# Two sums of output weights and all stores of plain gating weights placed in tile zero; GpSimd's sums cut into pieces of 256 columns and placed earlier

## The chip, the cores and the metric

The kernel runs on one core of a Trainium2 chip. The metric is the device time of one execution in microseconds; the time of a kernel is the median of its timed runs. One further execution of the kernel was taken by the hardware profiler, and all views of a profile below are of that one execution.

## What is computed

Attention inside chunks of 64 tokens (8 batches, 8 heads, 576 tokens of 64), then RMS norm and a SwiGLU layer over the 4608 tokens of 512 numbers:

```python
scores = scale * np.matmul(q_c, k_c.transpose(0, 1, 2, 4, 3))      # within a chunk
attn = softmax(scores);  out = np.matmul(attn, v_c)                # x: 4608 x 512
xn = x / rms * rms_g
g = xn @ w_gate                                                    # 512 x 1536
silu = g * (1.0 / (1.0 + np.exp(-g)))
val = xn @ w_val
return (silu * val @ w_out).astype(np.float32)                     # 1536 x 512
```

The weights arrive as 64-bit words and are made into float32 on the chip. Every matrix product is done in two-part numbers: each operand is split into a high and a low part, and three products of parts (high by high, high by low, low by high) are summed.

## The kernel before

**Tiles.** The 4608 tokens are nine tiles of 512. Tiles 0, 1 and 2 are computed plainly: for each of the 12 blocks `f` of 128 hidden units, 12 matmuls make the gate, 12 the value, SiLU and a product follow, and later the down product. Tiles 3 to 8 are taken in pairs by a seven-product scheme (`P1` to `P7`), which needs sums and differences of weight blocks; these are made once, stored in DRAM, and loaded again by each pair. Tile 0 keeps the names `acc`, `ps_g`, `ps_v` of its own; tiles 1 and 2 are one loop whose down products also use the seven-product scheme (`down_pair` with `b` = -1).

**What has to be prepared for the pairs.** There are six weight groups `i` (`NPR` = 6), each with three preparations:

- `save_up(i)` (L678) stores three plain weight blocks of the up side as they are: three DMAs of 512 KB from `parts` to the DRAM tensor `wsd`, all on SyncE's queue.
- `sides(i)` makes the four sums of the up side in a tile `ab`. It returns six functions, called at the half-steps `SIDE_AT[i] + SIDE_STEPS`: `whole` and `sums` on GpSimd (both through `total`, L693), then twice a `split` (two casts on ScalarE, `side`, L716, and two differences on VectorE, L717) and a `save` (four DMAs of 256 KB).
- `out_sides(i, home)` makes the sums of the output weights in a tile `w` and writes them back into `out_parts[i]`: `sums` (L657 and four L665, VectorE), `parts` (cast on ScalarE, L669; difference on VectorE, L670) and `store` (two DMAs of 512 KB to `wol`). They are called at `SUM_AT[i] + SUM_STEPS`.

**Attention ahead.** While tiles 1 and 2 are multiplied, the attention of units 4 to 9 (256 tokens each) is done in steps placed by `UNIT_AT`: load of queries and keys (`qk`, one buffer), scores on TensorE (L269), softmax (L341, L342, L348, L353 to L362), a trip of the exponentials through DRAM (`away_e`, then `eT`, one buffer), values on TensorE (L394), norm (`xu`, L408; the square on ScalarE, L464, which writes into `eT`; `ms` and `ri_t` on GpSimd, L466 and L467; L419) and a trip of the result through DRAM (`away_x`, back into `x`). At the turn from tile 1 to tile 2, L521 (ScalarE) and L522 (VectorE) split `x` into `xh` and `xl`.

**What sets the order.** Tile 0 is put in order by a scheduler with priorities. From tile 1 on the engines execute in the order in which the code is written: in tiles 1 and 2 there are 48 half-steps (two for each `f`), and a table gives the half-step at which a function is called. Every engine, and SyncE's queue of DMAs, takes its instructions strictly in turn. SyncE has eight semaphores for DMAs in turn, so each DMA also waits until the one issued eight before it has landed.

**Buffers.** The weight tiles, `ab` and the big `g` tiles share a pool of 18 buffers (`wts`), all of which the converted weights fill at the end of tile 0. The first buffer that comes free is that of `out_parts[0]`, when its `wol` store has landed; the first `ab` tile goes there.

Of the kernel before, what the change touches and what calls it, by code (L numbers as in the profile page):

```python
# [8 lines left out]
F32 = mybir.dt.float32  # L9
# [5 lines left out]
ALU = mybir.AluOpType  # L15
AX = mybir.AxisListType

P = 128
# [10 lines left out]
DM = 512  # L29
NDT = DM // P  # L30
DFF = 1536
NF = DFF // P
# [15 lines left out]
)  # L48
SIDE_AT = 6, 11, 15, 25, 29, 33
SIDE_STEPS = 0, 2, 4, 5, 6, 7  # L50
SUM_AT = 0, 3, 6, 11, 26, 32
SUM_STEPS = 0, 1, 3
SAVE_AT = 19, 22, 27, 31
LAST_HOME = 42
WO_AT = 36, 42
SPLIT_AT = 41, 45
# [13 lines left out]
KH = DM // 2  # L70
# [20 lines left out]
for p in DOWN:  # L91
    todo = [(p, i) for i in range(NPR)]
# [9 lines left out]
def tile_chunk_attn_swiglu(  # L102
# [40 lines left out]
    wp = last.open("wp", 3)  # L143
# [99 lines left out]
    def load_values(u):  # L243
        vt = io.tile([P, NPAIR, UT // CH, D], F32, tag="io", name="vt")
        nc.sync.dma_start(vt, v[u])
        for s in range(2):
            state[2 * u + s]["v"] = vt
# [280 lines left out]
    def behind(ins):  # L528

        info = mybir.DependencyInfo(mybir.DependencyClass.Sync, mybir.DependencyReason.DATA)  # L530
        tc.add_manual_dep(ins.ins, split_last[0].ins.name, info, reason="tokens are split first")
        return ins
# [114 lines left out]
    def out_sides(i, home):  # L647

        hi, lo = (out_parts[i][:, n].rearrange("p f (h c) -> p (f h) c", c=KH) for n in range(2))
        slots = wol_.rearrange("p (k i) (a c) -> p i a k c", i=NPR, a=2)[:, i]  # L650
        hi32, lo32 = hi.bitcast(F32), lo.bitcast(F32)
        ws = []

        def sums():
            w = home().tile([P, 4, KH], F32, tag="ab", bufs=1, name="w")
            ws.append(w)
            nc.vector.tensor_tensor(w, hi32, lo32, op=ALU.add)  # L657
            a11, a21, a12, a22 = (w[:, n] for n in range(4))
            for o, one, two, op in (
                (a22, a21, a22, ALU.add),  # L660
                (a21, a11, a21, ALU.subtract),
                (a11, a22, a11, ALU.subtract),
                (a12, a12, a11, ALU.subtract),
            ):
                nc.vector.tensor_tensor(o, one, two, op=op)  # L665

        def parts():
            w = ws[0]
            nc.scalar.copy(hi, w)  # L669
            nc.vector.tensor_tensor(lo, w, hi32, op=ALU.subtract)  # L670

        def store():
            for a, part in enumerate((hi32, lo32)):
                nc.sync.dma_start(slots[:, a], part)

        return [sums, parts, store]

    def save_up(i):  # L678

        for f, ps in enumerate(((P1, P2), (P4,))):  # L680
            part = conv_parts[2 * i + f].bitcast(F32).rearrange("p a m (h c) -> p h (a m) c", h=2)
            for h, p in zip((0, 1) if f == 0 else (1,), ps):
                nc.sync.dma_start(wsd[:, 7 * i + p].rearrange("p (n c) -> p n c", c=KH), part[:, h])
# [4 lines left out]
    def sides(i, st):  # L688

        at, ws = {}, []  # L690

        def total(out, one, two, op):
            return nc.gpsimd.tensor_tensor(out, one, two, op=op)  # L693

        def whole():
            ws = big([P, 2, 2, DM], F32, "ab")
            for f in range(2):
                hi, lo = (conv_parts[2 * i + f][:, n].bitcast(F32) for n in range(2))
                behind(total(ws[:, f], hi, lo, ALU.add))
                for half in range(2):  # L700
                    at[f + 1, half + 1] = ws[:, f, :, half * KH : (half + 1) * KH]

        def sums():
            total(at[2, 2], at[2, 1], at[2, 2], ALU.add)
            total(at[2, 1], at[1, 1], at[2, 1], ALU.subtract)
            total(at[1, 1], at[2, 2], at[1, 1], ALU.subtract)
            total(at[1, 2], at[1, 2], at[1, 1], ALU.subtract)

        forms = ((P7, (2, 1)), (P5, (2, 2))), ((P6, (1, 1)), (P3, (1, 2)))
        parts = {}  # L710

        def split(k):
            for p, n in forms[k]:
                w = at[n]
                part = parts[p] = st().tile([P, 2, KH], F32R, tag="side", bufs=4, name="side")
                nc.scalar.copy(part, w)  # L716
                nc.vector.tensor_tensor(w.bitcast(F32R), w, part.bitcast(F32), op=ALU.subtract)  # L717

        def save(k):
            for p, n in forms[k]:  # L720
                dst = wsd[:, 7 * i + p].rearrange("p (a m c) -> p a m c", a=2, m=2)
                nc.sync.dma_start(dst[:, 0], parts[p].bitcast(F32))
                nc.sync.dma_start(dst[:, 1], at[n])

        return [whole, sums, lambda: split(0), lambda: save(0), lambda: split(1), lambda: save(1)]

    def big(shape, dtype, name):
        return wts.tile(shape, dtype, tag="wts", name=name)
# [389 lines left out]
    for f in range(NF):  # L1118
        g = gated(f, CONVS[f % 2], conv_step)
        if f in (0, 5):  # L1120
            u = 2 + (f == 5)
            load_unit(u)
            load_values(u)
            sc = two_banks(ps_a, "ps_s")
            for i in (2 * u, 2 * u + 1):
                scores(i, sc)
            softmax_rows(u, sc)
        elif f in (2, 7):
            for i in (2 * u, 2 * u + 1):
                att_transpose(i)  # L1130
        elif f in (3, 8):
            o = two_banks(ps_a, "ps_o")
            for i in (2 * u, 2 * u + 1):
                att_values(i, o)
            norm_unit(u, o)
        if f % 2:
            save_out(f // 2)
        if f >= 10:
            save_up(f - 10)
        if f == NF - 1:  # L1140
            load_unit(4)
            x_transpose((0, 1))
        if prev is not None:
            down(acc, f - 1, *prev)
        prev = g
# [11 lines left out]
    st = [last.open("st", 1)]  # L1157
    xx = [x, None]
    at, down_at, wos, gs = {}, {}, {}, []
# [3 lines left out]
    def do(k, f):  # L1163
        if k >= 4 * NF:
            down_at.setdefault(2 * (k - 4 * NF), []).append(f)
        else:
            at.setdefault(max(k, 0), []).append(f)
# [12 lines left out]
    for n, u in enumerate(range(4, 10)):  # L1180
        todo = unit_steps(u, lambda n=n: xx[n >= 4])
# [3 lines left out]
    for i in range(NPR):  # L1185
        for k, f in zip(SIDE_STEPS, sides(i, lambda: st[0])):
            do(SIDE_AT[i] + k, f)
        for k, f in zip(SUM_STEPS, out_sides(i, lambda: st[0])):
            do(SUM_AT[i] + k, f)
        do(P5_AT[i], lambda i=i: less_first(i))  # L1190
        if i > 1:
            do(SAVE_AT[i - 2], lambda i=i: save_up(i))
    do(LAST_HOME, last_home)
    for n, k in enumerate(WO_AT):
        do(k, lambda n=n: wo_first(n))
# [3 lines left out]
    half = Steps(at)  # L1199
    room = []  # L1200
    for t in range(1, PLAIN):
        for f in range(NF):
            n = (t - 1) * NF + f
            if n < 4:
                tag = "gh" if n < 2 else "gl"
# [16 lines left out]
    for b in range(-1, NB):  # L1222
        t = PLAIN + 2 * b
        last_pair = b == NB - 1
        if b >= 0:
            at, down_at, wos, gs = {}, {}, {}, []
# [102 lines left out]
```

## Time and profile before

| | us |
|---|---|
| three timed runs | 921.89, 922.05, 923.31 (median 922.05) |
| the profiled execution | 919.45 |
| its span in the profile | 917.6 |
| TensorE busy in the span | 879.9 |
| VectorE / ScalarE / GpSimd busy | 688.9 / 436.7 / 162.5 |

Tile 0 runs to about 145 us, tiles 1 and 2 multiply their up side from there to 316 us, and their down products follow; the three pairs end the span. In a row of the timeline, the columns are the start, the duration of all the instructions in the row, the engine, the line, the operation with output and inputs, the count, and in brackets how long the engine stood idle before the row and what it waited for. In a row of the windows, each engine's busy time stands with its instruction count in brackets, then the clock granted to TensorE (1.00 is full speed), the mean busy share of the DMA engines, and GB/s.

### The profile page before, as it was taken

The page shows a single profiled execution, that of the slowest core. Times are in us where ns is not written, and L with a number is a line of the kernel's source. Part 1 is how long each engine was busy: PE and PEld are TensorE (multiplying, and loading weights), DVE is VectorE, ACT ScalarE, POOL GpSimd, SP SyncE. Part 2 cuts the span into 40 slices and gives each one's busy share as a digit, 9 for nine tenths or more (in the row PEclk, how much of TensorE's full clock was granted, in tenths as well). Part 3 has the DMA queues.
Part 4 walks back from the last instruction along what each step waited for, and adds up shares of the span by engine and source line. Part 5 has one row for each costly group of instructions (what it writes and reads, how often), then busy time and mean ns, then how long its engine had stood idle before and what let it go on. Part 6 is the DMA issues. An engine that isn't in the chain of part 4 may idle for free.

```text
span 917.6 us, 17117 instructions
## 1 busy us (share of the span) xinstructions
PE 879.9 (96%) x6792; PEld 719.4 (78%) x6792; DVE 688.9 (75%) x1083; ACT 436.7 (48%) x733; POOL 162.5 (18%) x153
## 2 busy tenths in 40 slices
PE   5799999979999999999999999999999999999998
PEld 4588878757777788888888788888878888888886
DVE  6999966878799597776666997776669874344885
ACT  5997944244444564333444654344446532212452
POOL 0100000276485100022221000221220002211000
PEclk9999999989999999999999999999999999999999
DMA  9698423759998997578888885688798867445623
GB/s 362 265 375 321 146 92 115 227 199 324 343 370 272 314 335 278 185 263 269 312 259 276 288 304 211 244 283 314 244 294 265 308 250 300 142 150 193 226 66 119
DMA packets 96513, 231.82 MB, mean 253 GB/s; under 512 B 7344, under 2 KB 63664, under 8 KB 81072
## 3 DMA queue, kind: packets, MB, share of 16 engines
q1 hardware_dynamic: 95376, 230.19, 72.1%
q8 instruction: 54, 0.88, 0.4%
q10 hardware_dynamic: 1056, 0.52, 0.2%
q14 instruction: 27, 0.22, 0.1%
HBM read 171.97 MB, written 58.72 MB: 251 GB/s over the span
## 4 chain that ended last, share of the span: by engine, by line
PE 71%; DVE 14%; ACT 7%; DMA 4%; issue 2%; POOL 1%; SPq 0%; ACTq 0%; DVEq 0%; POOLq 0%
PE ps_c L788 11%; PE ps_b L788 11%; PE ps_a L788 11%; PE ps_a L969 7%; PE ps_b L969 7%; PE ps_c L969 6%; PE ps_d L788 5%; PE ps_d L969 4%; PE ps_v L604 2%; DVE ab L717 2%; PE ps_g L604 2%; PE ps_s L269 1%; PE ps_o L394 1%; ACT e L309 1%; ACT parts L214 1%
## 5 line engine op out<-in xcount | busy, mean ns | idle before, releaser
L888 ACT CAST gh<-g 128x512 fp32r<-128x512 f32 x140 | 81.5, 619 | 75.5 <-PE ps_b L969 21.3
L889 DVE TENSOR_TENSOR gl<-g,gh 128x512 fp32r<-128x512 f32 x140 | 95.0, 686 | 29.7 <-ACT gh L888 28.7
L788 PE MATMUL ps_c<-xp,wr 128*128 128x512 f32 x432 | 104.6, 391 | 0.0
L788 PE MATMUL ps_b<-xp,wr 128*128 128x512 f32 x432 | 104.4, 391 | 0.0
L788 PE MATMUL ps_a<-xp,wr 128*128 128x512 f32 x432 | 103.6, 390 | 0.0
L788 PEld LDWEIGHTS ps_a<-xp,wr 128*128 128x128 f32 x432 | 80.9, 188 | 17.1 <-issue 0.3
L788 PEld LDWEIGHTS ps_c<-xp,wr 128*128 128x128 f32 x432 | 80.6, 188 | 17.1
L788 PEld LDWEIGHTS ps_b<-xp,wr 128*128 128x128 f32 x432 | 80.6, 188 | 16.9
L853 POOL TENSOR_TENSOR g<-c,c 128x512 f32<-128x512 f32 x18 | 23.3, 1294 | 358.3 <-DVE c L849 268.2
L604 PE MATMUL ps_v<-xh,parts 128*128 128x512 f32 x192 | 69.4, 416 | 0.0
L604 PE MATMUL ps_g<-xh,parts 128*128 128x512 f32 x192 | 65.0, 392 | 2.2 <-ACT sg L617 2.2
L969 PE MATMUL ps_a<-gh,wo 128*128 128x512 f32 x176 | 55.8, 389 | 0.0
L969 PE MATMUL ps_c<-gh,wo 128*128 128x512 f32 x160 | 51.1, 391 | 1.4 <-DVE gl L889 1.1
L788 PE MATMUL ps_d<-xp,wr 128*128 128x512 f32 x216 | 51.9, 389 | 0.0
L969 PE MATMUL ps_b<-gh,wo 128*128 128x512 f32 x160 | 50.5, 389 | 0.0
L788 PEld LDWEIGHTS ps_d<-xp,wr 128*128 128x128 f32 x216 | 40.5, 188 | 8.4
L931 DVE TENSOR_TENSOR g<-g 128x512 f32<-128x512 f32 x68 | 46.4, 682 | 0.0
L604 PEld LDWEIGHTS ps_v<-xh,parts 128*128 128x128 f32 x192 | 38.6, 201 | 9.1 <-issue 0.2
L604 PEld LDWEIGHTS ps_g<-xh,parts 128*128 128x128 f32 x192 | 36.0, 188 | 10.4 <-ACT sg L617 2.8
L829 ACT ACTIVATE c<-c 128x512 f32<-128x512 f32 x18 | 11.4, 633 | 67.7 <-DVE c L849 67.6
L838 DVE TENSOR_TENSOR u<-ps_b,p 128x512 f32<-128x512 f32 x36 | 24.0, 684 | 25.2 <-PE ps_b L788 24.0
L348 ACT ACTIVATE e<-e 128x512 f32<-128x512 f32 x28 | 17.5, 631 | 50.0 <-DVE e L342 50.0
(176 smaller groups left out, 1903.3 us busy)
## 6 DMA issues: line engine op xcount, KB each, us to landing
wr<-wsd SPq DMA_DIRECT2D x63, 1024.0 KB, 8.6
qk<-qk_dram SPq DMA_DIRECT2D x17, 1024.0 KB, 6.9
wo<-wol SPq DMA_DIRECT2D x16, 1024.0 KB, 8.4
raw<-w_up_dram SPq DMA_DIRECT2D x12, 1024.0 KB, 13.0
wo<-wod SPq DMA_DIRECT2D x12, 1024.0 KB, 9.8
vt<-v_dram SPq DMA_DIRECT2D x18, 512.0 KB, 6.1
wsd<-parts SPq DMA_DIRECT2D x18, 512.0 KB, 7.9
wo<-wol SPq DMA_DIRECT2D x16, 512.0 KB, 8.2
```

The lines of the kernel that those rows point to most:

```text
L214: nc.scalar.copy(parts[:, 0].rearrange("p i c -> p (i c)"), w)
L348: nc.scalar.activation(e, e, AF.Exp, scale=SCALE)
L604: nc.tensor.matmul(ps[k], a, b[dt], start=(dt == 0 and i == 0), stop=(dt == NDT - 1 and i == 2), skip_group_check=True,)
L717: nc.vector.tensor_tensor(w.bitcast(F32R), w, part.bitcast(F32), op=ALU.subtract)
L788: nc.tensor.matmul(ps, w[:, a, m, cols], xp[:, b, kt], start=start and kt == 0 and i == 0, stop=stop and kt == 1 and i == 2, skip_group_ch ...
L829: nc.scalar.activation(t, t if src is None else src, AF.Silu)
L838: nc.vector.tensor_tensor(kp["u2"], b["b"], kp["p1"], op=add)
L853: nc.gpsimd.tensor_tensor(g[1][1], kp["c22"], kept[0]["c22"], op=mult)
L888: nc.scalar.copy(gh, src)
L889: nc.vector.tensor_tensor(gl, src, gh.bitcast(F32), op=ALU.subtract)
L931: nc.vector.tensor_tensor(out, one, two, op=ALU.subtract)
L969: nc.tensor.matmul(ps[m][INTO[p]], w[:, m, a], parts[c], start=p in FROM and i == 0 and j == 0, stop=p in LAST and i == NPR - 1 and j == 2 ...
```

## The change

Four edits. `EARLY_SUMS` = 2: the whole of `out_sides(0)` and `out_sides(1)` is called in tile 0, at `f` = 9 and 10, with `w` in the pool of the weight conversion. All six `save_up` calls are made in tile 0, at `f` = 6 to 11; before, two were there and four at half-steps 19, 22, 27 and 31. GpSimd's `whole` and `sums` are cut into 256 columns: eight instructions where two of 1024 columns were, and eight where four of 2 x 256 were. `SIDE_AT` moves the six `sides` 5, 5, 4, 10, 4 and 3 half-steps forward, and two of the remaining `out_sides` 3 half-steps.

```diff
-SIDE_AT = 6, 11, 15, 25, 29, 33
+SIDE_AT = 1, 6, 11, 15, 25, 30
 SIDE_STEPS = 0, 2, 4, 5, 6, 7
-SUM_AT = 0, 3, 6, 11, 26, 32
+SUM_AT = 0, 0, 3, 8, 26, 32
 SUM_STEPS = 0, 1, 3
-SAVE_AT = 19, 22, 27, 31
+EARLY_SUMS = 2
...
         def sums():
-            w = home().tile([P, 4, KH], F32, tag="ab", bufs=1, name="w")
+            w = home().rearrange("p (n c) -> p n c", c=KH)
...
-                behind(total(ws[:, f], hi, lo, ALU.add))
                 for half in range(2):
-                    at[f + 1, half + 1] = ws[:, f, :, half * KH : (half + 1) * KH]
+                    cols = slice(half * KH, (half + 1) * KH)
+                    for m in range(2):
+                        behind(total(ws[:, f, m, cols], hi[:, m, cols], lo[:, m, cols], ALU.add))
+                    at[f + 1, half + 1] = ws[:, f, :, cols]
 
         def sums():
-            total(at[2, 2], at[2, 1], at[2, 2], ALU.add)
-            total(at[2, 1], at[1, 1], at[2, 1], ALU.subtract)
-            total(at[1, 1], at[2, 2], at[1, 1], ALU.subtract)
-            total(at[1, 2], at[1, 2], at[1, 1], ALU.subtract)
+            for m in range(2):
+                a = {n: w[:, m] for n, w in at.items()}
+                total(a[2, 2], a[2, 1], a[2, 2], ALU.add)
+                total(a[2, 1], a[1, 1], a[2, 1], ALU.subtract)
+                total(a[1, 1], a[2, 2], a[1, 1], ALU.subtract)
+                total(a[1, 2], a[1, 2], a[1, 1], ALU.subtract)
...
-        if f >= 10:
-            save_up(f - 10)
+        if f >= 6:
+            save_up(f - 6)
+        if f >= NF - 1 - EARLY_SUMS and f < NF - 1:
+            for todo in out_sides(f - NF + 1 + EARLY_SUMS, lambda: wp.tile([P, 2 * DM], F32, name="w")):
+                todo()
...
-        for k, f in zip(SUM_STEPS, out_sides(i, lambda: st[0])):
+        for k, f in () if i < EARLY_SUMS else zip(SUM_STEPS, out_sides(i, lambda: st[0].tile([P, 2 * DM], F32, tag="ab", bufs=1, name="w"))):
             do(SUM_AT[i] + k, f)
         do(P5_AT[i], lambda i=i: less_first(i))
-        if i > 1:
-            do(SAVE_AT[i - 2], lambda i=i: save_up(i))
```

Lines after the first edits are numbered four higher in the changed kernel (L716, L717 become L720, L721). TensorE's order is the same in both.

GpSimd, from the end of tile 0 into tile 1, as a difference of the two orders. `L693` is `total`; `ab<-parts` is `whole`, `ab<-ab` is `sums`; `ms` and `ri_t` belong to the norm of unit 4.

```order
 L512 TENSOR_TENSOR ri_u<-ss_u,mhalf 128x2 x2
-L693 TENSOR_TENSOR ab<-parts 128x1024 x2
+L693 TENSOR_TENSOR ab<-parts 128x256 x8
+L693 TENSOR_TENSOR ab<-ab 128x256 x8
+L693 TENSOR_TENSOR ab<-parts 128x256 x8
 L466 TENSOR_SCALAR ms<-ms 128x1
 L467 TENSOR_TENSOR ri_t<-ms,mhalf 128x1
```

All of side 0 and the first half of side 1 now stand ahead of the norm of unit 4; before, only the first half of side 0 did.

VectorE in tile 1, from the end of the softmax of unit 5 (`L362`) to the norm of unit 4 (`L408`) and on, before:

```order
L362 STREAM_TRANSPOSE e<-e 128x512
L657 TENSOR_TENSOR w<-parts 128x1024
L665 TENSOR_TENSOR w<-w 128x256 x4
L619 TENSOR_TENSOR gl<-ps_v,sg 128x512
L670 TENSOR_TENSOR parts<-w,parts 128x1024
L408 TENSOR_TENSOR xu<-ps_o,rs 128x16x32 x2
L619 TENSOR_TENSOR g<-ps_v,sg 128x512
L425 STREAM_TRANSPOSE xu<-xu 128x1024
```

The same place after:

```order
L362 STREAM_TRANSPOSE e<-e 128x512
L619 TENSOR_TENSOR gl<-ps_v,sg 128x512
L721 TENSOR_TENSOR ab<-ab,side 128x2x256 x2
L408 TENSOR_TENSOR xu<-ps_o,rs 128x16x32 x2
L657 TENSOR_TENSOR w<-parts 128x1024
L665 TENSOR_TENSOR w<-w 128x256 x4
L619 TENSOR_TENSOR g<-ps_v,sg 128x512
L670 TENSOR_TENSOR parts<-w,parts 128x1024
```

The third output sum (`L657`, `L665`, `L670`) no longer stands between the softmax of unit 5 and the norm of unit 4; it is earlier by one place of its kind, since the first two are in tile 0, and the next one stands behind the norm. Two pairs of differences of side 0 (`L721`) have come in ahead of the norm, one of them shown.

VectorE at the end of tile 0, before. `L200`, `L203` and `L220` convert the last weights; `L585` and `L590` are the gate's product and its low part for `f` = 9, 10 and 11.

```order
L200 SCALAR_TENSOR_TENSOR w<-raw,w 128x1024
L585 TENSOR_TENSOR sg<-ps_v,sg 128x512
L203 ISA w<-raw,w 128x2048
L590 TENSOR_TENSOR gl<-sg,gh 128x512
L220 TENSOR_TENSOR parts<-w,parts 128x1024 x2
L585 TENSOR_TENSOR sg<-ps_v,sg 128x512
```

After, from the second of the two `L220`:

```order
L220 TENSOR_TENSOR parts<-w,parts 128x1024
L665 TENSOR_TENSOR w<-w 128x256
L657 TENSOR_TENSOR w<-parts 128x1024
L585 TENSOR_TENSOR sg<-ps_v,sg 128x512
L665 TENSOR_TENSOR w<-w 128x256 x3
L590 TENSOR_TENSOR gl<-sg,gh 128x512
L665 TENSOR_TENSOR w<-w 128x256 x2
L670 TENSOR_TENSOR parts<-w,parts 128x1024
L665 TENSOR_TENSOR w<-w 128x256
L670 TENSOR_TENSOR parts<-w,parts 128x1024
L585 TENSOR_TENSOR sg<-ps_v,sg 128x512
```

Most of the two output sums (an `L657` and an `L665` stand further up) is done around the gate products of `f` = 10 and ahead of that of `f` = 11. On SyncE's queue, the twelve moved `save_up` DMAs stand between the stores of tile 0, the first two ahead of the load of the last raw weights; the four `wol` stores stand ahead of the stores of tile 0's output; and the load of unit 4's queries and keys stands behind nine of the twelve.

## The prediction

> **What bounds the kernel now.** I read the page's head first:
>
> ```profile
> span 917.6 us, 17117 instructions
> PE 879.9 (96%) x6792; PEld 719.4 (78%) x6792; DVE 688.9 (75%) x1083; ACT 436.7 (48%) x733; POOL 162.5 (18%) x153
> ```
>
> TensorE is busy 879.9 of 917.6 us, and the change gives it the same matmuls in the same order. So the time can move only by what TensorE waits, or by matmuls that run slowly. I went through TensorE's timeline for its waits; in the brackets stand the wait ahead of the row and what ended it. Between 145 and 316 us, the up side of tiles 1 and 2, where nearly all of the change lies, these are all of them:
>
> ```profile
> 182.71 0.50 PE L604 MATMUL ps_g<-xh,parts 128*128 128x512 f32 x1 [1.08 <-ACT sg L617]
> 188.59 0.27 PE L394 MATMUL ps_o<-vt,eT 64*32 64x64 f32 x2 [2.88 <-DMA eT<-away_e]
> 189.76 1.58 PE L394 MATMUL ps_o<-vt,eT 64*32 64x64 f32 x126 [0.89 <-DMA eT<-away_e]
> 200.76 0.33 PE L269 MATMUL ps_s<-qk 64*64 64x64 f32 x4 [2.31 <-DVE xu L408]
> 201.45 1.97 PE L269 MATMUL ps_s<-qk 64*64 64x64 f32 x60 [0.36 <-DVE xu L408]
> 217.18 1.35 PE L269 MATMUL ps_s<-qk 64*64 64x64 f32 x64 [2.08 <-DMA qk<-qk_dram]
> 234.32 0.50 PE L604 MATMUL ps_g<-xl,parts 128*128 128x512 f32 x1 [0.26 <-DVE xl L522]
> 270.75 0.33 PE L269 MATMUL ps_s<-qk 64*64 64x64 f32 x4 [1.85 <-DVE xu L408]
> 271.44 1.15 PE L269 MATMUL ps_s<-qk 64*64 64x64 f32 x60 [0.36 <-DVE xu L408]
> 290.58 0.50 PE L604 MATMUL ps_g<-xh,parts 128*128 128x512 f32 x1 [1.15 <-ACT sg L617]
> 307.64 0.27 PE L394 MATMUL ps_o<-vt,eT 64*32 64x64 f32 x2 [0.43 <-DMA eT<-away_e]
> 308.63 1.46 PE L394 MATMUL ps_o<-vt,eT 64*32 64x64 f32 x126 [0.72 <-DMA eT<-away_e]
> ```
>
> They add up to 14.37 us. I name them by place: B at 182.71 (1.08), C at 188.59 (2.88 + 0.89), A at 200.76 (2.31 + 0.36), D at 217.18 (2.08), E at 234.32 (0.26), F at 270.75 (1.85 + 0.36), G at 290.58 (1.15), H at 307.64 (0.43 + 0.72).
>
> Next come the windows behind these waits. After start:end and its length stand the busy times (and counts) of PE, PEld, DVE, ACT and POOL, then the granted clock, the DMA share and GB/s:
>
> ```profile
> 100.00:120.00 20.00, 20.00 (x152) 16.51 (x151) 19.08 (x28) 16.93 (x28) 0.02 (x1) 1.00 0.31 123
> 120.00:140.00 20.00, 18.46 (x85) 15.04 (x85) 12.60 (x16) 7.93 (x12) 1.67 (x1) 1.00 0.13 53
> 189.00:200.00 11.00, 8.70 (x150) 6.85 (x150) 9.90 (x8) 1.64 (x3) 8.95 (x5) 0.84 0.81 277
> 200.00:207.00 7.00, 5.88 (x77) 5.01 (x78) 5.47 (x8) 6.24 (x11) 5.12 (x6) 0.76 0.41 141
> 215.00:223.00 8.00, 5.92 (x78) 4.82 (x78) 7.49 (x13) 1.28 (x3) 5.72 (x5) 0.79 0.91 309
> 270.00:274.00 4.00, 2.89 (x68) 2.48 (x69) 3.86 (x8) 2.41 (x6) 2.21 (x4) 0.86 1.06 372
> 274.00:284.00 10.00, 10.00 (x40) 8.07 (x40) 10.00 (x7) 4.05 (x5) 9.77 (x6) 0.89 0.95 273
> 290.00:296.00 6.00, 5.42 (x24) 4.49 (x25) 5.86 (x14) 2.36 (x5) 0.00 (x0) 1.00 0.87 283
> ```
>
> Behind C, A, D and F, the four waits of 1.85 us or more, the clock was 0.84, 0.76, 0.79 and 0.86 to 0.89; behind G (1.15) it was 1.00. So a longer wait costs a second time. I price it as (1 − clock) × length: C 0.16 × 11 = 1.76, A 0.24 × 7 = 1.68, D 0.21 × 8 = 1.68, F 0.14 × 4 + 0.11 × 10 = 1.66; 6.78 in all. The stretch loses 14.37 + 6.78 = **21.15 us**. No more than that is to be had here.
>
> The Trainium skill (TensorE: Matmul & The Clock Gate, "What's actually happening") has the clock halved only after an idle window of about 3.4 us. By it none of these waits would slow a matmul, and the sum below would be smaller by its clock terms (1.76, 1.68 and two thirds of 1.66), about 4.5 us. The rows above disagree, with 0.76 behind a wait of 2.31 us, and I go by them.
>
> **The change, part by part.** *Two output sums leave tile 1.* VectorE, in tile 1, and what TensorE and SyncE did at that time:
>
> ```profile
> 153.76 1.22 DVE L657 TENSOR_TENSOR w<-parts 128x1024 f32<-128x1024 f32 x1
> 155.00 1.80 DVE L665 TENSOR_TENSOR w<-w 128x256 f32<-128x256 f32 x4
> 157.93 1.23 DVE L670 TENSOR_TENSOR parts<-w,parts 128x1024 fp32r<-128x1024 f32 x1 [0.52 <-ACT parts L669]
> 170.97 2.48 DVE L670 TENSOR_TENSOR parts<-w,parts 128x1024 fp32r<-128x1024 f32 x1 [1.91 <-ACT parts L669]
> 171.75 1.48 PE L394 MATMUL ps_o<-vt,eT 64*32 64x64 f32 x128
> 183.33 1.28 DVE L408 TENSOR_TENSOR xu<-ps_o,rs 128x512 f32<-128x512 f32 x2
> 185.46 1.74 SPq L377 DMA_DIRECT2D eT<-away_e  x4
> 200.02 1.28 DVE L408 TENSOR_TENSOR xu<-ps_o,rs 128x512 f32<-128x512 f32 x2
> ```
>
> Unit 4's attention matmuls end at 173.23, but its norm L408 starts at 183.33, because VectorE, strictly in turn, comes to it only then. One sum costs 1.22 + 1.80 + 1.23 = 4.25 us alone; the second one's L670 took 2.48, and it costs some 5.5. The third moves up into their place, so two of three are gone ahead of the norm: 9.7 us less. In come two pairs of differences, 4 × 0.64 = 2.6. Not all of the rest reaches the norm, since VectorE also waits for the softmax; I take 5 us sooner, 178 (5 to 7). C's load (185.46) follows that norm through ScalarE, so it lands near 183.5 instead of 188.5. Without B's wait TensorE wants it at 184.6: **C goes, and so does B**, whose SiLU waits in the same run of work. That is 1.08 + 3.77 + 1.76 = 6.61.
>
> A waits for the norm of unit 5 (200.02). Ahead of it stood the third sum's L657 and L665, 2.80 and 3.88 us in place of 1.22 and 1.80, beside GpSimd. The norm comes to 190 to 193; TensorE, without C, wants it at about 191.7. I leave half a us of A: 2.67 + 1.68 − 0.5 = 3.85 gone (bounds 0 and 4.35).
>
> *GpSimd's sums in pieces.* The pair of differences L717 beside GpSimd and alone, and GpSimd's groups (count, then busy us and mean ns):
>
> ```profile
> 251.13 2.31 DVE L670 TENSOR_TENSOR parts<-w,parts 128x1024 fp32r<-128x1024 f32 x1
> 257.81 5.25 DVE L717 TENSOR_TENSOR ab<-ab,side 128x512 fp32r<-128x512 f32 x2 [0.61 <-ACT side L716]
> 293.19 1.27 DVE L717 TENSOR_TENSOR ab<-ab,side 128x512 fp32r<-128x512 f32 x2
> ```
>
> ```profile
> 169.96 5.74 POOL L693 TENSOR_TENSOR ab<-parts 128x1024 f32<-128x1024 f32 x2 [48.29 <-DMA wol<-parts]
> 257.31 5.20 POOL L693 TENSOR_TENSOR ab<-parts 128x1024 f32<-128x1024 f32 x2
> L693 POOL TENSOR_TENSOR ab<-ab 128x512 f32<-128x512 f32 x24 | 35.2, 1466 | 1.7
> L693 POOL TENSOR_TENSOR ab<-parts 128x1024 f32<-128x1024 f32 x12 | 31.9, 2677 | 48.6 <-DMA wol<-parts 48.6
> L466 POOL TENSOR_SCALAR ms<-ms 128x1 f32<-128x1 f32 x28 | 8.9, 318 | 88.4 <-ACT eT L464 86.9
> ```
>
> Two differences take 1.27 us alone and 5.25 beside a pair of GpSimd sums of 5.20: VectorE is held until GpSimd's instruction is over. A side now costs GpSimd 2 × 2.68 + 4 × 1.47 = 11.2 us. After, it is 16 pieces: 0.67 each (2677 / 4) if nothing is paid per instruction, 0.91 if the 0.32 of a one-column instruction is paid each time; 10.7 to 14.6 a side. I take 0.73 (1466 / 2), 11.7. So GpSimd's own work grows by 0.5 us a side; it is idle 48 us ahead of its first sum, and that sum, waiting for the `wol` store, is able to start near 145 instead of 169.96, since those stores move into tile 0.
>
> The Trainium skill (SBUF — State Buffer, "Who interferes with whom") says that the ports which these two share are locked for a whole instruction and the second to come waits it out. The trace agrees (5.25 beside 5.20). By that rule a piece caps VectorE's wait at about 0.7 us.
>
> In tile 2 F hangs on a chain on VectorE from 247 to the norm at 270.02, with 5.25 for 1.27 and 2.31 for 1.23 in it: up to 5 us too much. If the pieces let VectorE between, F (2.21 + 1.66) goes, and with it G (1.15) and H (1.15), which follow in the same chain: 6.17. No trace of before shows pieces; the bounds are 0 and 6.17, and as the pairs alone give the larger part of the needed 2.2 us, I take two thirds: 4.1.
>
> *The half-steps.* The sides come up to five half-steps earlier, so later differences leave the neighbourhood of D and E, but D is a transfer:
>
> ```profile
> 208.46 8.59 DMA qk<-qk_dram
> ```
>
> From the norm at 200.02 over the issue to the landing at 217.05 run about 17 us now; in the changed kernel norm and TensorE both come earlier, by about the same. I leave D as it is (bounds 0 and +1.5). E: with TensorE 10 us ahead and VectorE 8 to 10, `xl` may be late by 0 to 2.3; I take 1.26, that is **1.0 more** than now.
>
> *Tile 0.* The two sums, 2 × 4.25 = 8.5 us of VectorE, come in ahead of the last gate products:
>
> ```profile
> 137.59 0.69 DVE L585 TENSOR_TENSOR sg<-ps_v,sg 128x512 f32<-128x512 f32 x1 [6.09 <-PE ps_v L563]
> ```
>
> VectorE idles 6.09 us right there, and 7.4 in the window 120:140; the last part may push this row by 2 us, and TensorE by none or all of it. I take **0.5** (bounds 0 and 3). The twelve `save_up` DMAs that move here (6.3 MB) meet a DMA share of 0.31 and 0.13; where they leave, up to 267 us, the windows nearest by have 0.91 to 1.06. Behind them on SyncE's queue stands unit 4's load of queries and keys, for which the idle DMA engines are the cover; without it each 512 KB at the 277 GB/s of 189:200 would be 1.9 us.
>
> **The sum:** 6.61 + 3.85 + 4.1 − 1.0 − 0.5 = 13.1 us less (13.06). Of the profiled execution's 919.45 us that leaves 906.4; it lies 2.6 below the median of 922.05, from which I get **909.0**.
>
> **The rivals.** *All waits go.* VectorE gains 5 us or more at each norm, D's transfer meets emptier DMA queues (twelve stores fewer), and nothing of the 21.15 is left: 900.9. Against it: the 8.59 us of D.
>
> *The pieces change nothing.* GpSimd issues the next piece at once, and VectorE stays out until the whole row of them is over, as between the two sums of 257.31, which held it for both. Then only B and C go, 6.6 us: 915.4. For it: L717 at 257.81 got through neither of two back-to-back sums.
>
> *The transfers set the pace.* SyncE issues in turn, eight DMAs in flight; if the units' loads are held by their order there, TensorE waits the same amount one place later: 922. Against it: C's load follows its norm within 2.2 us.
>
> *GpSimd falls behind* (slower). If each piece has to wait in turn for a VectorE instruction, of 0.64 to 1.28 us in the rows above, a side takes 16 × (0.73 + 0.64) = 22 us to 32. By the table four sides must be through by half-step 22 of tile 1; with 24 half-steps from 145 to 234, that is near 227, or 20.5 a side, and that is the point from which it decides. At 23 a side the fourth ends 10 us late, its differences stand on VectorE ahead of the next norm, and against the 6.6 of B and C that is 3.4 slower: 925.5. Against it: VectorE reads PSUM in much of its work, and is 25% idle. By the same rule of the Trainium skill, the lock holds in both directions, so it speaks for this rival too.
>
> **How the numbers follow.** Forecast 0.45 (909.0); all waits go 0.15 (900.9); pieces change nothing 0.22 (915.4); the transfers set the pace 0.07 (922); GpSimd behind 0.11 (925.5). The range from 900.0 to 918.5 takes in the first three with the unknowns of A, D, E and tile 0, and leaves out 0.18. A measurement of this kernel can tell some 0.2%, 1.8 us, from no change: faster 0.82, same 0.07, slower 0.11.
>
> **What would show it.** Right: no wait at B and C, L408 of unit 4 near 178, at most 0.5 at A and a clock of 1.00 there; differences beside GpSimd at 0.6 to 1.4 us each; D as now. Wrong: pieces that last 1.4 us or more on GpSimd's rows (GpSimd behind); pairs of differences still at 5 us (pieces change nothing); an attention unit waiting for `eT` or `qk` after its norm is early (transfers); a wait of TensorE for L585 or L590 at 137 to 141 above 0.5 us (tile 0's sums are not covered).

## The result, and the profile after

| | before | changed |
|---|---|---|
| median | 921.97 us (4 runs, 920.94 to 923.31) | 905.75 us (4 runs, 905.03 to 906.31) |
| ratio to before | | 0.9823, interval 0.9806 to 0.9840 |
| profiled execution: its time, its span | 919.45, 917.6 us | 906.16, 904.3 us |
| TensorE idle in 146 to 316 us | 14.37 us | 4.60 us |

The forecast was 909.0 us in a range of 900.0 to 918.5. The forecast lies 3 us above the measured time. That it came so close is luck: two terms of its sum, C and E, had the wrong sign, and C's miss of 7.1 us was made up by D, E and tile 2, which gave 3.8, 1.5 and 2.7 us more than I had forecast.

The head of the changed kernel's page:

```profile
span 904.3 us, 17163 instructions
PE 876.5 (97%) x6792; PEld 716.5 (79%) x6792; DVE 670.2 (74%) x1083; ACT 437.3 (48%) x733; POOL 173.3 (19%) x213
```

TensorE's timeline of the changed kernel has exactly one wait left between 145 and 316 us. It stands at C, the values of unit 5, which wait for the transposed `eT`:

```profile
188.96 0.29 PE L394 MATMUL ps_o<-vt,eT 64*32 64x64 f32 x2 [3.89 <-DMA eT<-away_e]
189.95 2.03 PE L394 MATMUL ps_o<-vt,eT 64*32 64x64 f32 x126 [0.71 <-DMA eT<-away_e]
```

The windows around it (PE, PEld, DVE, ACT and POOL busy, granted clock, DMA share, GB/s):

```profile
185.00:189.00 4.00, 0.11 (x2) 0.08 (x2) 1.35 (x3) 1.63 (x3) 3.77 (x6) 1.00 1.10 333
189.00:196.00 7.00, 6.29 (x138) 5.11 (x139) 3.69 (x6) 2.37 (x6) 6.83 (x10) 0.51 1.04 374
196.00:200.00 4.00, 4.00 (x55) 3.14 (x56) 0.72 (x2) 0.48 (x1) 3.60 (x7) 1.00 0.99 324
```

C did not go. It grew from 3.77 to 4.60 us, and the clock behind it was 0.51 for 7 us: 0.49 × 7 = 3.4 us more. TensorE waits with the DMA engines full (share 1.10), not empty.

To see what each place gave, I set the starts of TensorE's blocks of matmuls in the two traces beside each other. The matmuls are the same in the same order, so the difference of two starts changes only where one of the kernels waits or runs slowly. This is how far the changed kernel is ahead on entering and on leaving each place:

| place | ahead on entering | on leaving | gain | forecast |
|---|---|---|---|---|
| start, tile 0, unit 4 | 0 | −0.72 | −0.72 | −0.5 |
| B (182.7) | −0.72 | 0.53 | +1.25 | +1.08 |
| C (188.6) | 0.53 | −1.05 | **−1.58** | +5.53 |
| A (200.8) | −1.05 | 3.42 | +4.47 | +3.85 |
| D (217.2) | 3.42 | 7.23 | **+3.81** | 0 |
| E (234.3) | 7.23 | 7.71 | +0.48 | −1.0 |
| F (270.8) | 7.71 | 11.87 | +4.18 | F, G and H |
| G (290.6) | 11.87 | 13.07 | +1.20 | together |
| H (307.6) | 13.07 | 14.52 | +1.45 | +4.1 |
| from 316 us to the end | 14.52 | 13.4 | −1.1 | 0 |

Of the −0.72 ahead of B, 0.39 is there before tile 0's first gate matmul, where nothing was changed. Of the last line 0.65 us are two small waits at 454 and 462 us (0.27 and 0.38).

Why C stayed is to be read from the timeline of the changed kernel: the norm of unit 4 on VectorE, ScalarE's last use of the buffer, and SyncE's queue in the order in which it issues.

```profile
176.67 1.28 DVE L408 TENSOR_TENSOR xu<-ps_o,rs 128x512 f32<-128x512 f32 x2
178.04 0.63 ACT L464 ACTIVATE eT<-xu 128x512 f32<-128x512 f32 x1
177.98 0.54 SPq L239 DMA_DIRECT2D qk<-qk_dram  x1
178.61 0.62 SPq L726 DMA_DIRECT2D wsd<-side  x1
179.32 0.46 SPq L727 DMA_DIRECT2D wsd<-ab  x1
179.88 0.49 SPq L726 DMA_DIRECT2D wsd<-side  x1
180.47 0.63 SPq L727 DMA_DIRECT2D wsd<-ab  x1
181.44 3.80 SPq L377 DMA_DIRECT2D eT<-away_e  x4
```

The view of the tile `eT` in the same stretch gives the time from issue to landing of these loads:

```profile
DMA to landing us min/median/max: 4.7/6.8/7.0
```

The norm of unit 4 came at 176.67, a little sooner than forecast, and ScalarE was done with the buffer of `eT` at about 178.8. The load that needs that buffer stood in the queue behind 1 MB of queries and keys and four of side 0's stores (256 KB each; four others had gone out at 169 to 172). It was issued from 181.44 on and took 6.8 us to land; before, the same load took 2.7:

```profile
DMA to landing us min/median/max: 2.4/2.7/2.9
```

### The profile page after: what moved, and what is told of

It reads as the page before. It is cut to its first block, busy times and chain, and to the rows that moved or that the text cites. A ratio compares the mean times of both kernels' runs of the same rounds, so it can differ in the third digit from the quotient of the medians.

```text
span 904.3 us, 17163 instructions
## 1 busy us (share of the span) xinstructions
PE 876.5 (97%) x6792; PEld 716.5 (79%) x6792; DVE 670.2 (74%) x1083; ACT 437.3 (48%) x733; POOL 173.3 (19%) x213
## 4 chain that ended last, share of the span: by engine, by line
PE 78%; DVE 6%; issue 6%; ACT 4%; DMA 3%; POOL 1%; SPq 0%; ACTq 0%; DVEq 0%; POOLq 0%
PE ps_a L792 10%; PE ps_c L792 10%; PE ps_b L792 10%; PE ps_a L973 7%; PE ps_b L973 7%; PE ps_v L604 6%; PE ps_c L973 6%; PE ps_g L604 6%; PE ps_d L792 5%; PE ps_d L973 4%; PE ps_s L269 2%; PE ps_o L394 2%; PE ps_g L563 1%; DMA wr<-wsd 1%; PE ps_v L563 1%
## 5 line engine op out<-in xcount | busy, mean ns | idle before, releaser
L604 PE MATMUL ps_v<-xh,parts 128*128 128x512 f32 x192 | 67.0, 403 | 0.0
L693 POOL TENSOR_TENSOR ab<-parts 128x256 f32<-128x256 f32 x48 | 38.5, 839 | 23.6 <-DVE xl L522 23.6
## 6 DMA issues: line engine op xcount, KB each, us to landing
raw<-w_up_dram SPq DMA_DIRECT2D x12, 1024.0 KB, 13.3
```

Of the source, the lines that this page charges most:

```text
L604: nc.tensor.matmul(ps[k], a, b[dt], start=(dt == 0 and i == 0), stop=(dt == NDT - 1 and i == 2), skip_group_check=True,)
```

## The experiments

Twelve kernels ran, each with three timed rounds beside the kernel before. Its median was 922.0, 921.7 and 920.7 us in the three sets, so ratios are compared; a difference of two medians tells only the size.

| run | median, us | ratio to before (interval) |
|---|---|---|
| changed kernel | 905.75 | 0.9823 (0.9806 to 0.9840) |
| e1 whole pieces | 909.42 | 0.9868 (0.9845 to 0.9890) |
| e2 late saves | 906.81 | 0.9836 (0.9821 to 0.9851) |
| e3 late sides | 903.4 | 0.9797 (0.9782 to 0.9811) |
| e4 qk later | 905.89 | 0.9822 (0.9803 to 0.9841) |
| e5 pieces only | 916.02 | 0.9941 (0.9922 to 0.9959) |
| e6 sums only | 909.73 | 0.9869 (0.9850 to 0.9888) |
| e7 stores later | 906.19 | 0.9836 (0.9822 to 0.9851) |
| e8 side behind turn | 900.1 | 0.9778 (0.9758 to 0.9799) |
| e9 the same, whole pieces | 905.42 | 0.9828 (0.9811 to 0.9845) |
| e10 fourth side later | 900.61 | 0.9778 (0.9762 to 0.9794) |
| e11 the same as e8, late saves | 905.2 | 0.9821 (0.9801 to 0.9841) |
| e12 both behind | 904.31 | 0.9815 (0.9801 to 0.9830) |

**Theory and rival.** My theory after the result: the missing sums free the norms (B, A, D), the pieces free tile 2, and the sooner sides put their stores ahead of `eT`, which keeps C. The rival: the order of the sides freed tile 2, the emptier DMA queues freed D, and C belongs to the unit's own chain.

### Parts put back one at a time

e1 writes GpSimd's sums as before:

```diff
-                for half in range(2):
-                    cols = slice(half * KH, (half + 1) * KH)
-                    for m in range(2):
-                        behind(total(ws[:, f, m, cols], hi[:, m, cols], lo[:, m, cols], ALU.add))
-                    at[f + 1, half + 1] = ws[:, f, :, cols]
+                behind(total(ws[:, f], hi, lo, ALU.add))
+                for half in range(2):
+                    at[f + 1, half + 1] = ws[:, f, :, half * KH : (half + 1) * KH]
...
-            for m in range(2):
-                a = {n: w[:, m] for n, w in at.items()}
-                total(a[2, 2], a[2, 1], a[2, 2], ALU.add)
...
+            total(at[2, 2], at[2, 1], at[2, 2], ALU.add)
...
```

> The changed kernel with GpSimd's sums in instructions of 1024 and 512 columns again; all else as changed (905.75 us). If the pieces are what lets VectorE in, the waits of tile 2 that went (F, G and H: together 6.85 us by the starts of TensorE's rows) come back for the larger part, pairs of differences beside GpSimd take over 2.5 us again, and the time is 910 to 913. If the sooner half-steps and the missing sums alone freed VectorE, TensorE waits nowhere in tile 2 and the time is 905 to 907.

Slower than the changed kernel by the ratio (0.9868 against 0.9823, the intervals apart), 4.1 us by the ratios and 3.7 by the medians, so the pieces are worth that. The 909.42 lies between the two forecasts, and the pieces work at another place than I thought: by the starts of the blocks 1.9 us are lost at E, 1.0 at F and 0.45 at H. Rows of e1's TensorE and VectorE:

```profile
227.90 0.50 PE L604 MATMUL ps_g<-xl,parts 128*128 128x512 f32 x1 [1.66 <-DVE xl L522]
251.41 5.25 DVE L717 TENSOR_TENSOR ab<-ab,side 128x512 fp32r<-128x512 f32 x2 [0.61 <-ACT side L716]
260.95 1.28 DVE L717 TENSOR_TENSOR ab<-ab,side 128x512 fp32r<-128x512 f32 x2
```

The pair of 5.25 us is back, as expected, but the next norm now stands far enough behind it that F is 0.64 us only. In the changed kernel the same pair took:

```profile
250.59 1.84 DVE L721 TENSOR_TENSOR ab<-ab,side 128x512 fp32r<-128x512 f32 x2 [2.89 <-ACT side L720]
```

Over the whole kernel (group of that line, before and changed, busy us and mean ns), the differences cost VectorE 9.8 us less. In e1 they cost 22.9, so 5.1 of the 9.8 are the pieces:

```profile
L717 DVE TENSOR_TENSOR ab<-ab,side 128x512 fp32r<-128x512 f32 x24 | 27.6, 1188 | 5.7 <-ACT side L716 3.3 <-POOL ms L466 1.4 <-POOL ri_t L467 0.8
```

```profile
L721 DVE TENSOR_TENSOR ab<-ab,side 128x512 fp32r<-128x512 f32 x24 | 17.8, 780 | 9.6 <-ACT side L720 9.6
```

and GpSimd's pieces, 96 of 256 columns, take 0.81 and 0.84 us:

```profile
L693 POOL TENSOR_TENSOR ab<-parts 128x256 f32<-128x256 f32 x48 | 38.5, 839 | 23.6 <-DVE xl L522 23.6
L693 POOL TENSOR_TENSOR ab<-ab 128x256 f32<-128x256 f32 x48 | 38.5, 808 | 2.8
```

That is 8 × 0.84 + 8 × 0.81 = 13.2 us a side, inside my 10.7 to 14.6 and above the 11.7 that I took.

e2 puts the twelve stores back:

```diff
+SAVE_AT = 19, 22, 27, 31
...
-        if f >= 6:
-            save_up(f - 6)
+        if f >= 10:
+            save_up(f - 10)
...
+        if i > 1:
+            do(SAVE_AT[i - 2], lambda i=i: save_up(i))
```

> The changed kernel with the plain blocks of the last four pairs stored at half-steps 19, 22, 27 and 31 again, as before; all else as changed. If the emptier DMA queues are what took away the wait D for the queries and keys of unit 7 (2.08 us and 1.71 of slow matmuls), it comes back in part, with some of F and H: 907 to 910. If D went because the norm of unit 5 and its transfers are sooner, the time stays at 905 to 907. C, ahead of half-step 19, should not change in either.

Not to be told from the changed kernel. D did not come back, so the moved plain stores are not why it went. C did not stay as it was, however: in e2's profiled execution, the slowest of its four, it is 5.85 us for 4.60, behind the same DMAs in the same order, which took longer (`qk` 9.2 us for 7.0). So a C read from one execution is not sure to 1 us.

e3 has the sides at the old half-steps:

```diff
-SIDE_AT = 1, 6, 11, 15, 25, 30
+SIDE_AT = 6, 11, 15, 25, 29, 33
```

> The changed kernel with the sides at half-steps 6, 11, 15, 25, 29 and 33 again, as before; all else as changed. If side 0's stores (eight of 256 KB between 169 and 181 us) are what holds the load eT at C, the wait of 4.60 us and 3.4 of slow matmuls there goes (8 us), and what differences beside the norms give back decides between 899 and 905. If the unit's own chain holds that load, C stays and the time is 906 to 912, as the sides then collide later.

The time is 0.9797 of before, below the changed kernel's 0.9823, the intervals overlapping by 0.0005. TensorE's, SyncE's and VectorE's rows of e3:

```profile
173.42 1.29 DVE L408 TENSOR_TENSOR xu<-ps_o,rs 128x512 f32<-128x512 f32 x2 [1.41 <-PE ps_o L394]
184.44 1.48 PE L394 MATMUL ps_o<-vt,eT 64*32 64x64 f32 x128
175.56 1.75 SPq L377 DMA_DIRECT2D eT<-away_e  x4
221.45 0.50 PE L604 MATMUL ps_g<-xl,parts 128*128 128x512 f32 x1 [2.40 <-DVE xl L522]
```

C is gone without a trace: the load is issued at 175.56 instead of 181.44. Of these 5.9 us, 3.3 are the norm of unit 4 (173.42 for 176.67), ahead of which the differences of side 0 no longer stand, and the rest is the shorter queue. TensorE is then 7.9 us ahead of the changed kernel, and gives 2.7 back at E, where VectorE is late for the turn of the tile, and 2.1 at F and H. So **the sooner half-steps of the sides made C**, and they did not pay for it.

e5 and e6 each do one part alone in the kernel before: e5 has the pieces (the edit of e1 the other way round), e6 the sums in tile 0:

```diff
-SUM_AT = 0, 3, 6, 11, 26, 32
+SUM_AT = 0, 0, 3, 8, 26, 32
+EARLY_SUMS = 2
...
+        if f >= NF - 1 - EARLY_SUMS and f < NF - 1:
+            for todo in out_sides(f - NF + 1 + EARLY_SUMS, lambda: wp.tile([P, 2 * DM], F32, name="w")):
+                todo()
...
-        for k, f in zip(SUM_STEPS, out_sides(i, lambda: st[0])):
+        for k, f in () if i < EARLY_SUMS else zip(SUM_STEPS, out_sides(i, lambda: st[0].tile([P, 2 * DM], F32, tag="ab", bufs=1, name="w"))):
```

> The kernel before with one part of the change: GpSimd's sums in pieces of 256 columns; the order, the sums and the stores as before (922.0 us). If pieces let VectorE in wherever both work, the differences of 5.25 us in tile 2 fall to about 2 and F goes for the most part (it cost 4.2 us), with some of A: 915 to 918. If pieces are worth something only in the sooner order, 920 to 923. B and C, which stand behind the output sums, stay in both.

> The kernel before with one part of the change: the first two output sums in tile 0, and the places of the others as in the changed kernel; sides, pieces and stores as before. If the sums ahead of the norms are what made B, C and A, the norm of unit 4 comes by about 178 us, B (1.25 us) and C (5.5 with its slow matmuls) go and A shrinks: 909 to 915, of which a sooner TensorE may give back 2 to 4 us at E. If C needs emptier queues as well, it stays: 917 to 921.

The pieces alone are worth 5.7 us (F gone, C at 3.74 as it was; B, which the expectation left in place, went too, and D grew from 2.08 to 2.49), the sums alone 12. In e6 the norm of unit 4 comes at 173.44 and takes B, C, A **and D** with it, with stores and sides as before: D went because the norm of unit 5 and with it the load behind it come sooner, by more than TensorE: the norm by 14.1 us (185.94), the load's landing by 15.9, TensorE at the scores by 11.3. TensorE is 15 us ahead in e6 when it reaches E, and loses four of them there, waiting 2.38 us for `xl` at this row and running slowly behind it:

```profile
221.58 0.78 PE L605 MATMUL ps_g<-xl,parts 128*128 128x512 f32 x1 [2.38 <-DVE xl L523]
```

### What holds the load at C

e4 and e7 take one thing each from in front of the load in the changed kernel. e4 moves the load of unit 6's queries and keys, e7 the stores of side 0 (the stores alone; the splits, which the expectation also names, stay where they were); e12 does both.

```diff
-    (8, 14, 20, 16, 18, 20, 25, 27, 27, 28, 31),
+    (10, 14, 20, 16, 18, 20, 25, 27, 27, 28, 31),
```

```diff
-            do(SIDE_AT[i] + k, f)
+            do(SIDE_AT[i] + k + (i == 0 and k in (5, 7)), f)
```

> The changed kernel with one number changed: the load of unit 6's queries and keys (1 MB) stands at half-step 10 instead of 8, behind the load eT of unit 5. If eT waits for bytes ahead of it in the DMA queues, it lands some 3 us sooner, C falls from 4.60 us to about 1.5 and its slow matmuls by 1.7 to 3.4: 899 to 902. If eT is held by its place behind the four side stores in SyncE's order or by its own chain, C stays within 1 us and the time is 904 to 907. The scores of unit 6 (half-step 14, at 199.4 us) could wait for the later load: then A comes back by 1 to 3 us.

> The changed kernel with only side 0's two splits and their stores a half-step later (7 and 9 for 6 and 8), so that the second four stores stand behind the load eT of unit 5. If these stores ahead of it are what holds it, C falls from 4.60 us to under 1.5 and its slow matmuls go, 5 to 7 us; the sooner TensorE then meets E, where VectorE is late with xl by 2 to 2.5 us, as in the two runs in which C shrank: 900 to 904. If bytes in the queues hold it wherever they stand, C stays at 3 us or more: 904 to 907.

> The changed kernel with both edits that halved C: side 0's stores a half-step later and the load of unit 6's queries and keys at half-step 10, so that nothing large but the stores of the third output sum and unit 5's own transfers stands ahead of the load eT. If C is the time that bytes ahead of it in the queues take, the two gains add up (1.8 and 2.4 us of 4.6) and C falls to 0 to 0.6. If one and the same delay was removed twice, C stays at 1.5 to 2.5. The time says little, since E (2 to 3 us and its slow matmuls) gives it back: 902 to 906.

TensorE's waits in e4, in e7 and in e12, between 175 and 230 us:

```profile
186.57 0.27 PE L394 MATMUL ps_o<-vt,eT 64*32 64x64 f32 x2 [1.62 <-DMA eT<-away_e]
187.46 1.46 PE L394 MATMUL ps_o<-vt,eT 64*32 64x64 f32 x126 [0.62 <-DMA eT<-away_e]
208.31 1.27 PE L269 MATMUL ps_s<-qk 64*64 64x64 f32 x64 [1.49 <-DMA qk<-qk_dram]
225.59 0.50 PE L604 MATMUL ps_g<-xl,parts 128*128 128x512 f32 x1 [1.96 <-DVE xl L522]
```

```profile
187.50 0.27 PE L394 MATMUL ps_o<-vt,eT 64*32 64x64 f32 x2 [2.23 <-DMA eT<-away_e]
188.36 1.46 PE L394 MATMUL ps_o<-vt,eT 64*32 64x64 f32 x126 [0.59 <-DMA eT<-away_e]
223.27 0.49 PE L604 MATMUL ps_g<-xh,parts 128*128 128x512 f32 x1 [0.67 <-ACT xh L521]
226.15 0.50 PE L604 MATMUL ps_g<-xl,parts 128*128 128x512 f32 x1 [2.39 <-DVE xl L522]
```

```profile
208.50 1.89 PE L269 MATMUL ps_s<-qk 64*64 64x64 f32 x64 [4.33 <-DMA qk<-qk_dram]
225.82 0.50 PE L604 MATMUL ps_g<-xl,parts 128*128 128x512 f32 x1 [0.44 <-DVE xl L522]
```

C is 2.24 in e4, 2.82 in e7, and gone in e12: the two gains add up, so C was the load's place behind both. Its own flight went from 6.8 us to 3.9 in e4 and 3.4 in e12. In e7 it stayed at 6.8, and the load was issued 1.6 us sooner (179.89). In none of the three did the time follow. What TensorE gained at C it lost again at D or E, 906 to 904 us. The expectation of e4 for the time (899 to 902) and that of e7 (900 to 904) failed on this: E was named in e7's, and was priced too low, since slow matmuls came behind it. The C of 2.82 in e7 lies between that expectation's two cases. The wait that e4's expectation feared at A came at D.

### A better order

e8 is e3 with one number changed. The third side starts at 18 instead of 15, so that its second pair of differences stands behind all of `xl` and its first in between. (The expectation gives 23 and 25; the differences stand at 22 and 24, their stores at 23 and 25.)

```diff
-SIDE_AT = 1, 6, 11, 15, 25, 30
+SIDE_AT = 6, 11, 18, 25, 29, 33
```

> The changed kernel with the sides at 6, 11, 18, 25, 29 and 33: as in the run with the late sides (903.4 us), but the third from 15 to 18, so that its two pairs of differences stand behind the turn of the tile (half-steps 23 and 25). If VectorE's queue, and not the arrival of x, makes the wait E (2.40 us there), E falls to 0.5 or less and the time to 900.5 to 902, unless the later differences hold the norm of unit 7, which shows as a wait at TensorE between 240 and 260. If x itself is late, E stays at 2 us: 903 to 905.

900.1 us, 0.9778 of before, below the changed kernel with the intervals apart; those of e8 and e3 still overlap. E is 0, as VectorE now comes to `xl` ahead of the third side's differences, but for the last of its four parts, which stands behind the first pair. VectorE's rows of e3 and then of e8:

```profile
220.64 2.74 DVE L522 SCALAR_TENSOR_TENSOR xl<-x,g_col,xh 128x512 fp32r<-128x512 f32 x4
```

```profile
217.69 2.06 DVE L522 SCALAR_TENSOR_TENSOR xl<-x,g_col,xh 128x512 fp32r<-128x512 f32 x3
```

The one wait that TensorE has left between 145 and 316 us in e8 is F, with the clock at 1.00 behind it:

```profile
254.69 0.33 PE L269 MATMUL ps_s<-qk 64*64 64x64 f32 x4 [1.19 <-DVE xu L408]
255.28 1.15 PE L269 MATMUL ps_s<-qk 64*64 64x64 f32 x60 [0.27 <-DVE xu L408]
```

From e8 three more runs start. e9 has whole pieces again (the edit of e1), e10 has `SIDE_AT = 6, 11, 18, 26, 30, 33`, and e11 puts the twelve stores back (the edit of e2).

> The run with the sides at 6, 11, 18, 25, 29 and 33 (900.1 us) with GpSimd's sums in instructions of 1024 and 512 columns again. If the pieces are worth what they were in the changed kernel and in the kernel before (3.7 and 5.7 us), 903 to 906, with F as the wait that grows. If they are only worth something where a side stands beside a norm, 900 to 902.

> The same run with the fourth and fifth sides a half-step later (26 and 30 for 25 and 29), in pieces. F (1.46 us there) waits for the norm of unit 7, which stands on VectorE behind the second pair of differences of the fourth side (2.37 us beside GpSimd); that pair now stands behind the norm. If that pair is the cause, F goes and the time is 897.5 to 899.5; if the chain ahead of it is late anyway, F stays over 1 us and the time is 900 to 901.

> The run with the sides at 6, 11, 18, 25, 29 and 33 (900.1 us) with the plain blocks of the last four pairs stored at half-steps 19, 22, 27 and 31 again, as before. If the twelve stores hold the units' transfers once TensorE waits for nothing else, waits for eT or qk of 1 us and more come back between 200 and 300 us and the time is 902 to 905. If the transfers have room, as the run with only these stores put back says (906.8 against 905.75), it is 900 to 901.5.

e9 is 5.3 us slower than e8 (4.6 by the ratios), with the intervals apart. With nothing else late, the pieces are worth about what they were in the kernel before, and they work where I had put them, at F and behind it. Rows of e9:

```profile
242.74 4.24 DVE L717 TENSOR_TENSOR ab<-ab,side 128x512 fp32r<-128x512 f32 x2 [0.61 <-ACT side L716]
256.83 0.33 PE L269 MATMUL ps_s<-qk 64*64 64x64 f32 x4 [2.71 <-DVE xu L408]
276.67 0.50 PE L604 MATMUL ps_g<-xh,parts 128*128 128x512 f32 x1 [1.31 <-ACT sg L617]
```

e10 takes F away as expected, and TensorE waits 1.36 us at G and 1.63 at H instead: 900.61 where 897.5 to 899.5 was expected, no gain. e11 is slower than e8 in its timed runs (905.2 against 900.1, the intervals just apart), so the moved stores are worth something once the rest is not late; only part of it shows in its profiled execution (902.33 us, the lowest of its four), where H is 2.24 us. Where the rest goes stays open.

## Why the prediction was right, and where it was not

**What bounds the kernel: right.** TensorE's waits and slow matmuls between 145 and 316 us were 14.37 + 6.78 = 21.15 us; 4.60 + 3.4 = 8.0 are left. The difference of 13.1 is the forecast sum and nearly the 13.3 by which the span fell, but by luck: by the starts of the blocks, the places from B to H gave 15.2, and 1.8 were lost ahead of and behind them. The median fell by more, 16.2 us, since the profiled execution was 2.5 below the median before and 0.4 above it after.

**The sums that leave tile 1: right, and larger than forecast.** The norm came at 176.67 where I had 178. B and A went. Alone (e6) they bring it to 173.44, and with the sides late (e3) it is at 173.42: the sooner sides hold it up by 3.3 us, for which I had allowed 2.6. The sum whose L657 and L665 stood ahead of the norm of unit 5, which I called the third, is the fourth (193.39; the third is at 178.05); the term does not change by it.

**"C goes": wrong, by 7.1 us.** The step that failed is "C's load (185.46) follows that norm through ScalarE, so it lands near 183.5". It took the 5 us from the norm to the landing (183.33 to 188.5) from before, where they became 12 (176.67 to 189), and did not look at what the sooner half-steps had put ahead of the load on SyncE's queue: two times four stores of side 0, with the 1 MB of `qk` between. I had listed the queue's new order for the `save_up` stores and the `wol` stores only. e3, e4, e7 and e12 show it: in e4 and e7 one piece taken from in front of the load shortens C, and without both (e12), or with the sides late (e3), it is gone.

**"I leave D as it is": wrong, by 3.8 us.** I let the norm of unit 5 and TensorE come sooner by the same amount. The norm came 8.0 us sooner (192.00 for 200.02) and the load landed 17 us behind it, as before. TensorE reached the scores only 3.4 us sooner (211.7 for 215.1), and found the load there. Rows of the changed kernel, with the flight of that load:

```profile
192.00 1.29 DVE L408 TENSOR_TENSOR xu<-ps_o,rs 128x512 f32<-128x512 f32 x2 [1.93 <-PE ps_o L394]
203.05 0.38 SPq L239 DMA_DIRECT2D qk<-qk_dram  x1
```

```profile
DMA to landing us min/median/max: 5.6/5.6/5.6
```

e6 shows D gone by the sums alone, also with C gone and TensorE sooner; e2 shows that the moved plain stores have no part in it. Whether the two `wol` stores that stood right ahead of this load before (205.54) made its flight of 8.6 us longer than the 5.6 here is not separated.

**E: wrong in sign, by 1.5 us, for a reason that hangs on C.** TensorE was 7 us ahead there, not 10, as it had been held at C. Where C was gone or shorter (e3, e4, e6, e7), `xl` was late by 2.0 to 2.4 us, the upper end of the 0 to 2.3 that I gave; in e12, where D held TensorE for 4.33 us, by 0.44.

**Tile 2: right in direction, 6.85 for 4.1.** The pieces do what I took for likeliest: a pair takes 1.84 us where it took 5.25. But at F, G and H either the pieces or the sooner sides do most of it alone. By the starts of the blocks 5.4 us are gained there without the pieces (e1, which loses 1.9 at E besides), 4.8 with the sides late (e3), 6.85 with both, and nothing with neither (e6). In the order of e8 and in that of before, where the sides are late, it is the pieces (4.6 and 5.4 us in all by the ratios). The ground given for *The pieces change nothing* was misread: L717 at 257.81 did get through between the two back-to-back sums. Its first difference was over at 260.26, while the second sum ran until 262.50, so each difference waited out one sum:

```profile
257.81 2.45 DVE L717 TENSOR_TENSOR ab<-ab,side 128x512 fp32r<-128x512 f32 x1 [0.61 <-ACT side L716]
259.67 2.83 POOL L693 TENSOR_TENSOR ab<-parts 128x1024 f32<-128x1024 f32 x1
```

**Tile 0: right.** In all 0.72 us were lost up to B, 0.39 of them ahead of the first gate matmul; 0.5 was forecast, and TensorE waited nowhere between 125 and 146 us. *GpSimd falls behind* did not happen: 13.2 us a side, far from 20.5. *The transfers set the pace*, given 0.07, is the rival that came true at one place, C, and it would have had more of my chance if I had followed all the stores through the queue.

## What to carry to other kernels

- When work is moved sooner, list every DMA that it issues and what then stands behind them in the same in-order queue. The engine work fitted; its stores took the place of the wait that was removed.
- A gain at one place arrives only if the next place is ready for a sooner TensorE. Three edits that shortened C by 1.8 to 4.6 us moved the time by 1.4 us at most. With C gone by the late sides and E freed by one number (e8) the time followed, to 900.1.
- Splitting an instruction that locks out another engine pays by what it frees on the path, not by the busy time that it saves. In three orders (e1, e5, e9) the same edit took 5.1, 7.2 and 10.0 us from VectorE's differences, and 4.1, 5.4 and 4.6 us by the ratios from the time, sizes that these runs cannot tell apart.

## What the runs showed of the hardware

The slow matmuls come in fixed steps of time. In windows of 1 us of the kernel before (the clock is the number before the last two), the slow stretches behind C, A, D and F begin in these:

```profile
190.00:191.00 1.00, 1.00 (x124) 1.00 (x101) 1.00 (x1) 0.95 (x2) 0.92 (x2) 0.97 1.05 360
194.00:195.00 1.00, 1.00 (x5) 0.84 (x4) 1.00 (x1) 0.00 (x0) 1.00 (x1) 0.82 0.95 331
201.00:202.00 1.00, 0.64 (x24) 0.58 (x24) 0.30 (x1) 1.00 (x4) 0.37 (x2) 0.59 0.00 0
218.00:219.00 1.00, 1.00 (x30) 0.84 (x21) 0.97 (x2) 0.00 (x0) 0.92 (x2) 0.62 0.76 243
272.00:273.00 1.00, 1.00 (x41) 0.89 (x31) 0.93 (x3) 1.00 (x4) 0.92 (x2) 0.93 1.03 371
```

Within them the clock is 1.00 or 0.50, so 0.97 means that the last 0.06 us were at half: they begin at 190.94, 201.18, 218.24 and 272.86. The first ends at 194.36, 3.42 us later. The distances between the beginnings are 10.24, 17.06 and 54.62 us, that is 3, 5 and 16 times 3.41. So the clock changes on a grid of 3.41 us, and a wait costs 1.7 us more (half of 3.41), or a multiple of it, or nothing. Behind the 4.60 us at C in the changed kernel it was two steps (0.51 over 7 us). A wait of 1.96 us at E in e4 was followed by a clock of 0.57 over 4 us; one of 2.40 in e3 and one of 2.82 at C in e7 cost nothing more:

```profile
226.00:230.00 4.00, 4.00 (x12) 3.17 (x11) 2.13 (x4) 0.00 (x0) 0.00 (x0) 0.57 0.88 294
```

```profile
221.00:226.00 5.00, 4.55 (x20) 3.78 (x21) 2.98 (x5) 0.00 (x0) 0.00 (x0) 1.00 0.89 288
```

What tells them apart is mostly the idle time within one step of the grid, not the length of the wait. In ten of the fourteen traces such an onset lies between 146 and 316 us, and the grid can be counted from it. Of the steps there that ran at full clock, all fourteen with 1.95 us or more of TensorE idle were followed by half clock and none with 1.63 or less was; of the four between 1.66 and 1.81 us one was. What decides between those stays open.

The Trainium skill (TensorE: Matmul & The Clock Gate, "What's actually happening") gives a free-running window of 3413 ns. The rows agree with that. It also has the clock halved after an idle window; F was preceded by one with only 1.66 of its 3.41 us idle (269.45 to 272.86, with waits of 1.85 and 0.36, of which the first began ahead of it), so a window about half idle was enough there, though the one from 184.12 to 187.53, idle for 1.81 us from the start of C's wait, left the clock at 1.00. The measurement decides.
